# The last expert's second layer: two products of the second row block moved ahead, and the last row block computed in two column parts

## The chip, the cores and the metric

The kernel runs on one core of one Trainium2 chip. The metric is the device time of one execution in microseconds (us), taken as the median of several runs. A profile is one execution recorded by the hardware profiler; its span runs from the first to the last instruction.

## What is computed

A gated linear attention block feeds a mixture-of-experts block without dropped tokens. Cut to what matters:

```python
# attention: q, k, v, alpha of shape (4, 8, 768, 48)
state = alpha_t * state + k_t (outer) v_t ;  y_t = q_t @ state
x = y as rows: (3072, 384)

# experts: w_gate (384, 8), w1 (8, 384, 1024), w2 (8, 1024, 384)
logits = x @ w_gate ; expert_idx = argmax(logits) ; gate_w = softmax(logits)[expert_idx]
for e in range(8):                      # rows sorted by expert
    h = maximum(x_sorted[lo:hi] @ w1[e], 0.0)
    y_sorted[lo:hi] = h @ w2[e]
out = gate_w[:, None] * y_sorted[inv_perm]     # (3072, 384), float32
```

The change touches only `h @ w2[e]` of the last expert that is worked on.

## The kernel before, in words

The first part of the kernel (to about 150 us) computes the attention and routes each token to an expert. The rest goes through eight places, one expert at each. A place has a fixed number of rows: 424 less 8 for each place before it, so that the last place has 368. The experts with more tokens come first. Rows are gathered from DRAM, go through layer 1 (384 to 1024, with relu) and layer 2 (1024 to 384), and are scattered to the output by an indirect DMA on the GpSimd queue (`put`, L1080). Rows beyond a place's fixed number are dealt with in a loop at the end (L1344), which the kernel enters only if a count that it loads there is above zero.

All of this is under a manual schedule: each engine does its instructions in the order in which the code issues them, and waits are put in where data demand them.

Layer 1 (`layer1`, L948) uses a product scheme with seven products in place of eight. It works in four steps `a` of 128 columns of the hidden layer, and each step fills the hidden blocks `a` and `a + 4` of `g["h"]` (the tile `h_sb`, blocks 0 to 7). The last products, `P3` and `P4` of step 3, finish blocks 3 and 7. Their results go through VectorE (L192) and ScalarE (the relu of L978 and L982) before they are there. To have work for TensorE meanwhile, `ahead` (the `begin` of L1274) is called just before those last two products.

At places 0 to 6 the second layer uses the seven-product scheme again. The last place does it plainly, with rows as the output's partitions: blocks of 128, 128 and 112 rows (`blocks(g)`), each a sum over the eight hidden blocks `f`, with 128 columns of `h` as the stationary operand and 384 columns of `w2` as the moving one (`rows_layer2`, L1114). A float32 product of this kind is two matmul instructions with a weight load each, so that a row block has 16 of them. `ready` (L1112) lists the six hidden blocks that are there early: all but 3 and 7.

The order on TensorE at the last place:

1. The six ready products of row block 0, into a bank of the pair `pC` (tile `tp`), from `begin` (L1276).
2. `P3` and `P4` of step 3 of layer 1 (L969).
3. Hidden blocks 3 and 7 of row block 0 (L1329).
4. All eight of row block 1, into the pair `pA` (tile `sA`).
5. All eight of row block 2, into the pair `pB` (tile `sB`).

`bank` (L839) deals out PSUM banks by name, two for each name in turn. The name `y` stands for two banks that the attention used and that only the first place's early rows use later.

After each row block `scatter` (L1071) copies the sum from PSUM to a row tile `zo` (one of four buffers) and issues the put. Row blocks 0 and 1 are copied whole by ScalarE (L1077). Row block 2 is `shared`: VectorE copies the first 192 columns (L1074) and ScalarE the other 192 (L1075). Ahead of row block 0's copy, ScalarE's queue holds three copies of the place before (`z_whole`, L1106), whose puts are ahead of the last three on the GpSimd queue.

Of the kernel before, what the change touches and what calls it, by code (L numbers as in the profile page):

```python
# [8 lines left out]
F32 = mybir.dt.float32  # L9
# [11 lines left out]
def kernel(  # L21
# [29 lines left out]
    nc = tc.nc  # L51
    B, H, S, D = q.shape
    C = 128
# [4 lines left out]
    Dm = H * D  # L58
    E = moe_w_gate.shape[1]
    F = moe_w1.shape[2]  # L60
    FB = F // C
# [10 lines left out]
    NJ = 4  # L72
# [115 lines left out]
    FH = FB // 2  # L188
# [171 lines left out]
    def weights(i, layer):  # L360
        if 0 < i < E:
            ex = nc.sync.value_load(pd["xe"][0:1, i : i + 1], min_val=0, max_val=E - 1)
            groups[i][f"w{layer}"] = fetch(ex, layer)

    def blocks(g, by=1):
        return [(j, min(C, -(-(g["n"] - j * C) // by) * by)) for j in range(-(-g["n"] // C))]

    def gather(g):
        if "xg" not in g:
            g["xg"] = xg_pool.tile([C, NJ, Dm], F32, name="xg")  # L370
        for j, r in blocks(g, 16):
            nc.gpsimd.indirect_dma_start(  # L372
                out=g["xg"][:r, j, :], out_offset=None,
                in_=x_d[:, :], in_offset=bass.IndirectOffsetOnAxis(ap=g["gi"](j, r), axis=0),
            )
# [13 lines left out]
    with tc.tile_pool(name="ld", bufs=6) as ld, \  # L389
         tc.tile_pool(name="work", bufs=2) as work:  # L390
        st = {s: {} for s in range(NT)}
        y = ps.tile([C, 2, 512], F32, name="y")
# [441 lines left out]
    wk = ctx.enter_context(tc.tile_pool(name="moe_wk", bufs=1))  # L834
# [4 lines left out]
    def bank(n):  # L839
        b = banks[n]  # L840
        if len(b) < 2:
            t = pairs[n][len(b)]
            if n == "y":
                b.append(y[:, t, :])
            else:
                b.append(ps.tile([C, 512], F32, name=t, bufs=2 if t == "tp" else 1)[:])
        else:
            b.append(b.pop(0))
        return b[-1]
# [15 lines left out]
    def x_halves(g, copy=nc.scalar.copy):  # L865

        g["xt"] = wk.tile([C, NJ, 2 * DB, C], U16, name="xt")
        for j, r in blocks(g, 16):
            t = wk.tile([C, 2, Dm], U16, name="xh", bufs=4)
            copy(t[:r], g["xg"][:r, j, :].bitcast(U16).rearrange("p (c h) -> p h c", h=2))  # L870
            nc.sync.dma_start(g["xt"][:, j, :, :r], t[:r].rearrange("p h c -> p (h c)"), transpose=True)
            yield

    def x_whole(g, *js):
        if 0 in js:
            g["xT"] = wk.tile([C, DB, CAP0 + 8], F32, name="xgT")
        to = halves(g["xT"])
        for j, r in blocks(g):
            if j not in js:
                continue  # L880
            nc.scalar.copy(  # L881
                to[:, :, :, j * C : j * C + r], g["xt"][:, j].rearrange("p (h a) t -> p h a t", h=2)[:, :, :, :r],
            )
# [184 lines left out]

        return p1, rest

    def scatter(g, j, r, zp, shared=False):  # L1071
        zo = wk.tile([C, Dm], F32, name="zo", bufs=4)
        if shared:
            nc.vector.tensor_copy(zo[:r, : Dm // 2], zp[:, : Dm // 2])  # L1074
            nc.scalar.copy(zo[:r, Dm // 2 :], zp[:, Dm // 2 :])  # L1075
        else:
            nc.scalar.copy(zo[:r], zp)  # L1077
        put(g, j, r, zo)

    def put(g, j, r, zo):  # L1080
        ins = nc.gpsimd.indirect_dma_start(  # L1081
            out=out[:, :], out_offset=bass.IndirectOffsetOnAxis(ap=g["si"](j, r), axis=0),
            in_=zo[:r], in_offset=None, bounds_check=N - 1, oob_is_err=False,
        )
        if g["apart"]:
            ins = getattr(ins, "ins", ins)
            tc.declare_no_dep(ins, group="rows_out", reason="disjoint rows")
            tc.add_to_no_dep_group("rows_out", ins)
# [20 lines left out]
            )  # L1109
            put(g, j, r, zo)  # L1110

    ready = [f for f in range(FB) if f % FH < FH - 1]  # L1112

    def rows_layer2(g, j, fs):  # L1114

        r = min(C, g["n"] - j * C)
        if fs[0] == ready[0]:
            g["z"] = bank("p" + "CAB"[j])
        for f in fs:
            nc.tensor.matmul(  # L1120
                g["z"][:r, :Dm], lhsT=g["h"][:, f, j * C : j * C + r], rhs=g["w2"][:, f, :],
                start=(f == ready[0]), stop=(f == FB - 1), skip_group_check=True,
            )

    def plain(g):
# [77 lines left out]
    def early_layer2(j, fs):  # L1203

        if 0 in fs:
            eg["z"] = bank("y" if j else "pA")
        for f in fs:
            nc.tensor.matmul(
                eg["z"][:, :Dm], lhsT=eg["h"][:, f, j * C : (j + 1) * C], rhs=groups[0]["w2"][:, f, :],
                start=(f == 0), stop=(f == FB - 1),  # L1210
            )
        if FB - 1 in fs:
            yield
            scatter(eg, j, C, eg["z"][:, :Dm])
        yield

    def rest_layer1(g, beside, rows):
        n = g["n"]
        g["h"] = wk.tile([C, FB, CAP0], F32, name="h_sb")
        for f in range(FB):  # L1220
            hp = bank("p" + "CBA"[f % 3])
            for a in range(DB):
                nc.tensor.matmul(
                    hp[:, :n], lhsT=g["w1"][:, a, f * C : (f + 1) * C], rhs=g["xT"][:, a, :n],
                    start=(a == 0), stop=(a == DB - 1),
                )
            if f % 2:
                nc.vector.tensor_scalar_max(g["h"][:, f, :n], hp[:, :n], 0.0)
                next(beside, None)
            else:  # L1230
                nc.scalar.activation(g["h"][:, f, :n], hp[:, :n], AF.Relu)
                next(rows)
# [26 lines left out]
    def beside(i):  # L1259

        work = [z_halves(groups[i - 1])]
        if i == 1:
            work += [weight_sums(groups[1], 2, nc.vector)]
        while work:
            work = [w for w in work if next(w, w) is not w]
            yield

    for i, g in enumerate(groups):
        nxt = groups[i + 1] if i + 1 < E else None
        rest = []  # L1270

        last = i == E - 1

        def begin():  # L1274
            if last:
                rows_layer2(g, 0, ready)  # L1276
            else:
                p1, tail = layer2(g)
                p1()
                rest.append(tail)  # L1280

        if last:

            nc.gpsimd.drain()
        if i:
            layer1(g, beside(i), begin, last)
        else:
            rest_layer1(g, pl, x_halves(nxt))

            x_whole(nxt, 0, 1)  # L1290
            for _ in early_layer2(1, range(FH, FB)):
                pass
            x_whole(nxt, 2, 3)
            weights(1, 2)
        weights(i + 2, 1)
        if i + 2 < E:
            gather(groups[i + 2])
        if i == 0:
            for _ in x_halves(groups[2], nc.gpsimd.tensor_copy):
                pass  # L1300

        def ahead(*layers):
            if nxt:
                for layer in layers:
                    for _ in weight_sums(nxt, layer, nc.vector):
                        pass

        def turned():
            z_whole(groups[i - 1], nc.scalar.copy, 0, 1)
            yield  # L1310
            if nxt:
                row_sums(nxt)
            z_whole(groups[i - 1], nc.scalar.copy, 2)
            z_whole(groups[i - 1], nc.vector.tensor_copy, 3)
            yield
            if i + 2 < E:
                for _ in x_halves(groups[i + 2]):
                    pass
            yield

        between = turned()

        if 0 < i < E - 1:
            x_whole(nxt, *range(NJ))
        if last:
            for _ in between:
                pass
            for j, r in blocks(g):
                rows_layer2(g, j, (*([] if j == 0 else ready), FH - 1, FB - 1))  # L1329
                scatter(g, j, r, g["z"][:r, :Dm], shared=j == NJ - 2)  # L1330
        elif i:
            rest[0](lambda: ahead(*((1,) if i == E - 2 else (1, 2))), between)
        else:
            ahead(1)
            rest_layer2(g, 0)
            row_sums(nxt)
            rest_layer2(g, 1)
            rest_layer2(g, 2)
        weights(i + 2, 2)
# [4 lines left out]
    with tc.If(nx > 0):  # L1344
        with tc.For_i(0, nx, 1) as i:
# [13 lines left out]
            g = dict(n=C, w1=fetch(ex, 1), w2=fetch(ex, 2), gi=lambda j, r: gi[:, 0:1], si=lambda j, r: si[:, 0:1], apart=False)  # L1359
# [32 lines left out]
```

## Time and profile before

| | |
|---|---|
| median of 3 runs | 392.02 us (391.99 to 392.81) |
| the profiled execution's own time | 391.55 us |
| its span | 389.8 us |
| mean granted TensorE clock | 0.996 |
| instructions | 9094, of them 3378 matmuls |
| TensorE busy | 380.1 us (98% of the span) |
| VectorE, ScalarE, GpSimd busy | 210.0, 230.2, 149.2 us |

In the timeline, a row is a group of instructions that follow each other: its start, the time from the first start to the last end, engine, line, operation, output and inputs by the program's names, shapes and count; in brackets, the idle time before it and what ended that. "PE" is TensorE's matmuls, "PEld" its weight loads, which go on beside them. Matmuls are pipelined: each lasts longer than the distance between two starts, and the modelled end of the last one closes a group.

The part that the change touches begins at about 367 us of the span and ends with it.

### The profile page before, as it was taken

The page shows a single profiled execution, that of the slowest core. Times are in us where ns is not written, and L with a number is a line of the kernel's source. Part 1 is how long each engine was busy: PE and PEld are TensorE (multiplying, and loading weights), DVE is VectorE, ACT ScalarE, POOL GpSimd, SP SyncE. Part 2 cuts the span into 40 slices and gives each one's busy share as a digit, 9 for nine tenths or more (in the row PEclk, how much of TensorE's full clock was granted, in tenths as well). Part 3 has the DMA queues.
Part 4 walks back from the last instruction along what each step waited for, and adds up shares of the span by engine and source line. Part 5 has one row for each costly group of instructions (what it writes and reads, how often), then busy time and mean ns, then how long its engine had stood idle before and what let it go on. Part 6 is the DMA issues. An engine that isn't in the chain of part 4 may idle for free.

```text
span 389.8 us, 9094 instructions
## 1 busy us (share of the span) xinstructions
PE 380.1 (98%) x3378; PEld 324.1 (83%) x3378; DVE 210.0 (54%) x649; ACT 230.2 (59%) x521; POOL 149.2 (38%) x203
## 2 busy tenths in 40 slices
PE   7999999999999999999999999999999999999994
PEld 4678888888888886899889889979979979979852
DVE  5554667676676566726843663582582581552200
ACT  4576677777755431635665775675675665673540
POOL 6546464789768204257050043035025022021041
PEclk9999999999999999999999999999999999999998
DMA  8999998998994315789949459858758766801311
GB/s 169 200 201 218 203 231 194 231 218 208 244 229 136 107 42 193 149 312 250 305 117 248 85 205 235 137 197 193 188 197 206 178 203 166 157 20 38 61 63 52
DMA packets 156545, 68.08 MB, mean 175 GB/s; under 512 B 139339, under 2 KB 150722, under 8 KB 156500
## 3 DMA queue, kind: packets, MB, share of 16 engines
q1 hardware_dynamic: 151396, 57.77, 62.6%
q0 software_dynamic: 3408, 9.64, 8.3%
q8 instruction: 27, 0.44, 0.5%
q10 hardware_dynamic: 1696, 0.08, 0.3%
q14 instruction: 18, 0.15, 0.1%
HBM read 49.00 MB, written 9.58 MB: 150 GB/s over the span
## 4 chain that ended last, share of the span: by engine, by line
PE 77%; issue 15%; POOL 2%; DMA 2%; ACT 1%; DVE 1%; POOLq 0%; SPq 0%; ACTq 0%; DVEq 0%
PE tp L1051 7%; PE tp L489 6%; PE y L539 6%; PE sA L502 6%; PE x L969 4%; PE sA L969 4%; PE x L576 4%; PE sA L1034 4%; PE tp L969 3%; PE cum L969 3%; PE sB L969 3%; PE y L529 3%; PE x L1034 3%; PE tp L1034 2%; POOL out_dram L1081 2%
## 5 line engine op out<-in xcount | busy, mean ns | idle before, releaser
L1081 POOL DMA_INDIRECT out_dram<-zo,sp x25 | 26.0, 1042 | 137.5 <-ACT zo L1106 127.0
L479 POOL TENSOR_TENSOR kqb<-k_sb,icp 128x384 f32<-128x384 f32 x23 | 23.0, 1000 | 30.2 <-PE y L550 12.5
L1051 PE MATMUL tp<-h_sb,w 128*128 128x416 f32 (+5 forms) x96 | 33.9, 496 | 0.0
L502 PE MATMUL sA<-qT,kT 48*128 48x128 f32 x192 | 27.7, 284 | 0.9 <-DVE qT L493 0.9
L502 PE MATMUL sB<-qT,kT 48*128 48x128 f32 x192 | 27.7, 285 | 0.0
L372 POOL DMA_INDIRECT xg<-x_rows,gp x25 | 23.9, 954 | 10.0 <-issue 6.6
L1051 PEld LDWEIGHTS tp<-h_sb,w 128*128 128x128 f32 x96 | 18.0, 190 | 10.3 <-issue 3.7
L489 PE MATMUL tp<-ident,kqb 128*128 128x128 f32 x192 | 26.3, 280 | 0.2 <-DVE kqb L479 0.2
L502 PEld LDWEIGHTS sA<-qT,kT 48*128 48x128 f32 x192 | 23.1, 187 | 3.8 <-ACT kT L495 1.1
L980 ACT ACTIVATE h_sb<-h_sb 128x208 f32<-128x208 f32 (+6 forms) x28 | 10.3, 366 | 25.3 <-DVE h_sb L192 25.3
L192 DVE TENSOR_TENSOR h_sb<-cum,u 128x208 f32<-128x208 f32 (+6 forms) x28 | 10.1, 359 | 27.2 <-PE cum L969 20.7
L558 ACT COPY yT<-y 128x512 f32<-128x512 f32 x24 | 14.1, 587 | 17.8 <-PE y L550 7.9
L192 DVE TENSOR_TENSOR h_sb<-sB,u 128x208 f32<-128x208 f32 (+6 forms) x28 | 10.1, 359 | 26.1 <-PE sB L969 18.7
L479 POOL TENSOR_TENSOR kqb<-q_sb,cp 128x384 f32<-128x384 f32 x23 | 23.0, 1002 | 1.7 <-DMA q_sb<-in_q_dram 1.3
L969 PE MATMUL tp<-xgT,w 128*128 128x208 f32 (+6 forms) x112 | 23.1, 329 | 0.0
L489 PEld LDWEIGHTS tp<-ident,kqb 128*128 128x128 f32 x192 | 20.5, 140 | 3.2 <-issue 0.7
L502 PEld LDWEIGHTS sB<-qT,kT 48*128 48x128 f32 x192 | 23.1, 187 | 0.0
L510 DVE TENSOR_TENSOR dA<-sA,cmask 128x512 f32<-128x512 f32 x24 | 16.5, 688 | 10.2 <-PE sB L502 10.0
L195 DVE TENSOR_TENSOR th<-h_sb,th 128x208 f32<-128x208 f32 (+5 forms) x48 | 17.3, 361 | 8.1 <-ACT h_sb L982 8.1
L881 ACT COPY xgT<-xt 128x768 uint16<-128x768 uint16 (+6 forms) x25 | 20.8, 925 | 0.4 <-DMA xt<-xh 0.4
L576 PE MATMUL x<-iw,yT 128*64 128x104 f32 x368 | 20.8, 255 | 0.1
L1106 ACT COPY zo<-zr 128x768 uint16<-128x768 uint16 (+2 forms) x20 | 20.0, 1054 | 0.0
(302 smaller groups left out, 1029.0 us busy)
## 6 DMA issues: line engine op xcount, KB each, us to landing
w<-in_moe_w_dram SPq DMA_DIRECT2D x14, 1536.0 KB, 8.2
x_rows<-xs SPq DMA_DIRECT2D x24, 192.0 KB, 3.4
v_sb<-in_v_dram SPq DMA_DIRECT2D x10, 384.0 KB, 5.0
k_sb<-in_k_dram SPq DMA_DIRECT2D x9, 384.0 KB, 7.0
q_sb<-in_q_dram SPq DMA_DIRECT2D x9, 384.0 KB, 5.2
a_sb<-in_alpha_dram SPq DMA_DIRECT2D x7, 384.0 KB, 4.1
a_sb<-in_alpha_dram SPq DMA_DIRECT2D x10, 192.0 KB, 3.8
w<-in_moe_w_dram SPq DMA_DIRECT2D x6, 256.0 KB, 3.1
```

The costliest lines, as they stand in the source:

```text
L192: eng.tensor_tensor(out, a, b, op=ALU.add)
L372: nc.gpsimd.indirect_dma_start(out=g["xg"][:r, j, :], out_offset=None, in_=x_d[:, :], in_offset=bass.IndirectOffsetOnAxis(ap=g["gi"](j, r) ...
L479: eng.tensor_tensor(by_half(kq[:, i]), d[n].rearrange("s (a p) d -> s a p d", a=2), d[e][:].rearrange("s (a p d) -> s a p d", a=2, p=NP), ...
L489: nc.tensor.transpose(tp[:, p, :], pair(kqb[s % 3][:, i], p), ident[:])
L502: nc.tensor.matmul(t[:, p, :], lhsT=d["kT"][r : r + D, p, :], rhs=d["qT"][r : r + D, p, :], start=True, stop=True,)
L539: nc.tensor.matmul(yv(g)[o : o + D, j, :], lhsT=d["v"][:, g * NP + p, :], rhs=d["d" + "AB"[g]][:, p, :], start=(s < B and j == 0), stop=Tr ...
L576: nc.tensor.matmul(d["x"][o : o + HC, m, : D2 + E], lhsT=d["yT"][:, m // 2, m % 2, o : o + HC], rhs=iw[:, m, :], start=True, stop=True,)
L881: nc.scalar.copy(to[:, :, :, j * C : j * C + r], g["xt"][:, j].rearrange("p (h a) t -> p h a t", h=2)[:, :, :, :r],)
L969: nc.tensor.matmul(out, lhsT=ops[n_][0], rhs=ops[n_][1], start=first and n_ == names[0], stop=True, skip_group_check=True,)
L1034: nc.tensor.matmul(out, lhsT=lhs, rhs=rhs, start=first and f == 0, stop=True, skip_group_check=True)
L1051: nc.tensor.matmul(d2[:, :n], lhsT=w2[:, f, 2 * C :], rhs=h[:, f, :n], start=(f == 0), stop=(f == FB - 1),)
L1081: ins = nc.gpsimd.indirect_dma_start(out=out[:, :], out_offset=bass.IndirectOffsetOnAxis(ap=g["si"](j, r), axis=0), in_=zo[:r], in_offset= ...
```

## The change

- `scatter` loses its `shared` variant: every call copies the whole row block on ScalarE.
- `rows_layer2` keeps a sum for each row block (`g["z", j]` in place of `g["z"]`) and takes a bank name and a range of columns.
- At the last place, products 0 and 1 of row block 1 are issued before products 3 and 7 of row block 0; then row block 0 is copied and put, and the remaining six products of row block 1 follow.
- Row block 2 is computed in two parts: its first 256 columns into `pB` over all eight hidden blocks, copied by VectorE, and then its last 128 columns into the second bank of `y` over all eight, copied by ScalarE. Both copies go to the same `zo`, and one put follows.

```diff
-    def scatter(g, j, r, zp, shared=False):
+    def scatter(g, j, r, zp):
         zo = wk.tile([C, Dm], F32, name="zo", bufs=4)
-        if shared:
-            nc.vector.tensor_copy(zo[:r, : Dm // 2], zp[:, : Dm // 2])
-            nc.scalar.copy(zo[:r, Dm // 2 :], zp[:, Dm // 2 :])
-        else:
-            nc.scalar.copy(zo[:r], zp)
+        nc.scalar.copy(zo[:r], zp)
         put(g, j, r, zo)
...
-    ready = [f for f in range(FB) if f % FH < FH - 1]
-
-    def rows_layer2(g, j, fs):
+    late = [FH - 1, FB - 1]
+    ready = [f for f in range(FB) if f not in late]
+
+    def rows_layer2(g, j, fs, at=None, c0=0, c1=Dm):
 
         r = min(C, g["n"] - j * C)
         if fs[0] == ready[0]:
-            g["z"] = bank("p" + "CAB"[j])
+            g["z", j] = bank(at or "p" + "CA"[j])
         for f in fs:
             nc.tensor.matmul(
-                g["z"][:r, :Dm], lhsT=g["h"][:, f, j * C : j * C + r], rhs=g["w2"][:, f, :],
-                start=(f == ready[0]), stop=(f == FB - 1), skip_group_check=True,
+                g["z", j][:r, c0:c1], lhsT=g["h"][:, f, j * C : j * C + r], rhs=g["w2"][:, f, c0:c1],
+                start=(f == ready[0]), stop=(f == late[-1]), skip_group_check=True,
             )
...
         if last:
             for _ in between:
                 pass
-            for j, r in blocks(g):
-                rows_layer2(g, j, (*([] if j == 0 else ready), FH - 1, FB - 1))
-                scatter(g, j, r, g["z"][:r, :Dm], shared=j == NJ - 2)
+
+            b_ = blocks(g)
+            rows_layer2(g, 1, ready[:2])
+            rows_layer2(g, 0, late)
+            scatter(g, *b_[0], g["z", 0][: b_[0][1], :Dm])
+            rows_layer2(g, 1, ready[2:] + late)
+            scatter(g, *b_[1], g["z", 1][: b_[1][1], :Dm])
+
+            j, r = b_[2]
+            zo = wk.tile([C, Dm], F32, name="zo", bufs=4)
+            for n_, c0, c1, copy in (("pB", 0, 2 * C, nc.vector.tensor_copy), ("y", 2 * C, Dm, nc.scalar.copy)):
+                rows_layer2(g, j, ready + late, n_, c0, c1)
+                copy(zo[:r, c0:c1], g["z", j][:r, c0:c1])
+            put(g, j, r, zo)
```

More of the change, by code (lines that the diff above doesn't have):

```diff
@@ L1282 @@
         if last:
+            assert len(blocks(g)) == 3
             nc.gpsimd.drain()
```

## The prediction

> **What bounds the kernel now.** I read the page first: where the time goes, and on which engine.
>
> ```profile
> span 389.8 us, 9094 instructions
> PE 380.1 (98%) x3378; PEld 324.1 (83%) x3378; DVE 210.0 (54%) x649; ACT 230.2 (59%) x521; POOL 149.2 (38%) x203
> PEclk9999999999999999999999999999999999999998
> ```
>
> TensorE is busy for 98% of the span at full clock. So in the middle of the kernel only less TensorE work or fewer TensorE gaps count. After the last matmul it is a chain of other engines that counts. The change touches one gap and that last chain. The page's own chain ends in long "issue" pieces and says little here, so the timeline of the last 24 us is what I work from, first around the gap.
>
> ```profile
> 366.92 3.57 PEld L1120 LDWEIGHTS tp<-w,h_sb 128*128 128x128 f32 x12
> 367.07 4.03 PE L1120 MATMUL tp<-w,h_sb 128*128 128x384 f32 x12
> ...
> 371.57 0.79 PE L969 MATMUL cum<-t,w 128*128 128x184 f32 x4
> 371.77 0.33 ACT L978 ACTIVATE h_sb<-x 128x184 f32<-128x184 f32 x1 [3.71 <-PE x L969]
> ...
> 372.19 0.81 PE L1120 MATMUL tp<-w,h_sb 128*128 128x384 f32 x2
> 372.39 0.35 DVE L192 TENSOR_TENSOR h_sb<-cum,u 128x184 f32<-128x184 f32 x1 [3.95 <-PE cum L969]
> 372.78 0.51 ACT L982 ACTIVATE h_sb<-h_sb 128x368 f32<-128x368 f32 x1 [0.68 <-DVE h_sb L192]
> ...
> 373.34 0.30 PEld L1120 LDWEIGHTS tp<-w,h_sb 128*128 128x128 f32 x2 [0.95 <-ACT h_sb L982]
> 373.34 0.91 PE L1120 MATMUL tp<-w,h_sb 128*128 128x384 f32 x2 [0.34 <-ACT h_sb L982]
> ...
> 374.09 0.81 PE L1120 MATMUL sA<-w,h_sb 128*128 128x384 f32 x2
> ```
>
> The reader is to see one stall: hidden block 7 goes from the last layer-1 product (cum) through VectorE and ScalarE, whose relu ends at 372.78 + 0.51 = 373.29. TensorE has only product 3 (372.19) to fill that time, so product 7 starts at 373.34. Its stationary operand is the relu's output, so even the weight load waits. Next, the end of the kernel.
>
> ```profile
> 379.25 5.32 PE L1120 MATMUL sB<-w,h_sb 128*112 128x384 f32 x16
> 379.49 0.48 ACT L1077 COPY zo<-sA 128x384 f32<-128x384 f32 x1 [3.12 <-PE sA L1120]
> 380.25 0.99 POOL L1081 DMA_INDIRECT out_dram<-zo,sp  x1 [0.83 <-ACT zo L1077]
> 384.66 0.36 DVE L1074 COPY zo<-sB 112x192 f32<-112x192 f32 x1 [11.92 <-PEq L1344]
> 385.06 0.32 ACT L1075 COPY zo<-sB 112x192 f32<-112x192 f32 x1 [5.08 <-DVE zo L1074]
> 385.65 0.95 POOL L1081 DMA_INDIRECT out_dram<-zo,sp  x1 [4.41 <-ACT zo L1075]
> ```
>
> The two half copies run one after the other: ScalarE's is released by VectorE's. The last matmul ends at 379.25 + 5.32 = 384.57, the second copy at 385.06 + 0.32 = 385.38; so 0.81 us pass between them, and then the put, its landing and the closing of the program up to 389.8.
>
> **What the Trainium skill says.** "TensorE: Matmul & The Clock Gate", section "Step-by-step: what each phase is for", says that the next stationary operand loads while the present matmul runs. The trace agrees: in the rows above, 16 products with 16 loads take no longer than their streaming. The same page, "LDWEIGHTS (loading the stationary operand)", prices a load by its columns over 1.2, which is 107 ns for 128; the trace records 190 ns (177 for the 112 rows of block 2), and I use the distances between starts below. "PSUM — Partial Sum Buffer", "PSUM bank collisions raise a hardware error", says that two engines must not be in one bank and the same partitions at once. That is one reason for the half copies to stand in line (both read sB; they also write one zo). After the change the two copies read two banks.
>
> **Part 1, two products ahead.** Sixteen products of 384 columns take 5.32 us, of which the last takes 0.486 (a matmul's own duration in the rows of this line), so starts are (5.32 - 0.486) / 15 = 0.322 apart. From 372.19, the four instructions of products 3 and 7 would hand over to row block 1 at 372.19 + 4 x 0.322 = 373.48. It starts at 374.09: 0.61 us are lost. (0.34 are shown as idle; the rest is the drain of the product before and 0.10 of weight load in the open: 0.590 for the first product after the wait, where the others have 0.486.) With the change, products 0 and 1 of row block 1 run from 372.19 to 373.48, product 3 to 374.12, then product 7. Its weight load can start with its predecessor's start, near 373.80, half a microsecond after the relu is done. The whole 0.61 goes. The moved products need hidden blocks 0 and 1, there for long, and a bank of the pair pA: sA, whose last reader before was a relu at 366.34. So no new wait. What gets later is row block 0: done at about 374.9 in place of 374.25, but ScalarE is in three copies of the place before until 375.9, so its copy doesn't move. Row block 1 ends 0.61 earlier; its put moves from 380.25 to 379.64, behind row block 0's, which the GpSimd queue holds until 379.42: cover of 0.2, and four microseconds more before the last put. No DMA issue is moved past another, and SyncE's queue isn't touched. Gain: 0.61; if the load stayed in the open, 0.51.
>
> **Part 2, row block 2 in two parts.** It now takes 16 x 0.322 = 5.16 us. After the change it is 16 instructions of 256 columns and 16 of 128, with twice the weight loads. Both widths are in the trace elsewhere.
>
> ```profile
> 144.69 1.46 PE L671 MATMUL sB<-k_sb,w 128*128 128x256 f32 x6
> ```
>
> ```profile
> 59.83 0.82 PE L489 MATMUL tp<-ident,kqb 128*128 128x128 f32 x6
> ```
>
> ```profile
> 68.97 0.37 PE L275 MATMUL x<-pr,ones_sq 128*128 128x8 f32 x2
> ```
>
> The last of a group lasts its own duration, which each line's list gives (0.379, 0.273, 0.256). 256 columns: (1.46 - 0.379) / 5 = 0.216. 128 columns: six transposes, (0.82 - 0.273) / 5 = 0.109; but their loads are of the shorter kind (140 ns). The ordinary float32 load stands in the third row: two products of only 8 columns are 0.37 - 0.256 = 0.11 apart, so loads can follow each other at that distance. The cost of a narrow product lies between its streaming, 128 / 384 x 0.322 = 0.107 (nothing lower, as every column must pass), and 0.107 + 0.190 = 0.297, a load wholly in the open. I take 0.110. The sum is 16 x 0.216 + 16 x 0.110 = 5.22: a cost of 0.06.
>
> **Part 3, the copies.** VectorE's copy of 256 columns starts when the first part is complete. By its rows of 192 columns (0.358) and 512 (0.678) it lasts 0.42, beside the second part's 16 x 0.11 = 1.76: hidden, with over a microsecond to spare; without cover it would cost the 0.42. Behind it on VectorE stand only the load of the overflow count and the end. ScalarE's copy of 128 columns is, from 0.319 for 192 and 0.479 for 384, 0.266 long. It starts 0.08 after the last matmul, as at row block 1 (379.41 to 379.49). So 0.08 + 0.27 = 0.35 in place of 0.81: a gain of 0.46, with 0.42 to 0.50 as ends. The matmul's drain after its start distance is the same for either width (0.486 - 0.322, 0.273 - 0.109). The bank of y was last read near 166 us, and zo's buffer belonged to a put issued at 375.79, whose landing (median 2.7 us) is long past.
>
> **Part 4, after the copies.** The put follows the copy by 0.27 and takes 0.95, as before; the GpSimd queue has been idle since 381.24. "DMA: Bandwidth & Descriptors", "Anatomy of one DMA — SWDGE (gpsimd) path", puts about 2 us of fixed time on such a DMA; the trace has a median of 2.7 from issue to landing. All of that moves with the put and none of it is shortened.
>
> **Sum.** -0.61 + 0.06 - 0.46 = -1.01 us. The profiled execution took 391.55 (its span of 389.8 and 1.75 around it) and would take 390.54. The median of the runs shown is 392.02, 0.47 above it; with the same step it becomes 391.0.
>
> **Rivals.**
>
> A, *one half only*: the stall goes but the tail stays (ScalarE's copy still held back by VectorE or the new bank), or the reverse. 392.02 - 0.61 + 0.06 = 391.5, or 392.02 + 0.06 - 0.46 = 391.6. For it: the two copies share zo, and a wait for a whole tile is possible. Against it: VectorE's copy is over 1 us earlier than ScalarE's, so even that wait is met.
>
> B, *slower: the weight loads come into the open*. A narrow product streams for 0.107, less than the 0.177 that its load lasts in the record. If a load can't start before the load before it is through, or isn't hidden at all, every one of the 16 narrow products pays. Fully open: 16 x 0.177 = 2.8 us, so 392.02 - 1.07 + 2.8 = 393.8. It decides from 1.07 / 16 = 0.067 per product, a distance of 0.174. For it: loads are recorded longer than the product, and the stall above shows 0.10 of one. Against it: 0.11 for both kinds of load in the rows above.
>
> C, *no change that shows*: the tail is set by something that doesn't move, such as the landing of the last put, whose time varies. 392.0. Against it: nothing follows the last put but the program's end, and it all waits for it.
>
> **How the numbers follow.** Main case 0.82, A 0.08, B 0.05, C 0.05. By the unknown terms alone (stall 0.51 to 0.61, narrow products 0.107 to 0.112, tail 0.42 to 0.50) the main case gives 390.9 to 391.2. The three runs and the profiled one lie between 391.55 and 392.81, so a median moves by some 0.3, which makes 390.6 to 391.4. The range of 390.5 to 391.7 takes in A too; outside lie B, C and the rest of the scatter. A measurement tells 0.2% from no change, here 0.78 us, a line at 391.24. Of the main case about nine tenths lie below it (0.73), of A a quarter (0.02): faster 0.75. B counts as slower but for its mild end: 0.04. The rest, 0.21, is within 0.2%.
>
> **What would show it.** In the profile after: no wait of TensorE for the relu of L982 (0.34 before) and no gap before product 7; 16 narrow products in about 1.92 us (15 x 0.11 + 0.273), and 3.6 for the wide ones; VectorE's last copy ended before the last matmul; ScalarE's last copy ended about 0.35 after it; span near 388.8. Narrow products 0.17 or more apart would make the prediction wrong, and so would a last put that starts less than 0.8 earlier against the last layer-1 product (371.57 before).

## The result, and the profile after

The changed kernel takes 391.42 us (median of 22 runs); the kernel before takes 392.12 in the same number of runs. The ratio of the two is 0.9975, with a 95% interval of 0.9966 to 0.9983: 0.98 us less, between 0.67 and 1.33. The forecast was 1.01 less. One execution of the changed kernel took 1345.99 us, for a reason that no run shows, and the ratio leaves it out. The profiled execution took 390.48 us against 391.55, with a span of 388.8 us against 389.8.

One stretch can be compared from trace to trace without the scatter of what lies ahead of it: from the start of the last layer-1 products (four matmuls into `cum`, L969, at 371.57 before and at 371.52 after) to the end of the span. The first column of these rows is the stretch, and the number after it its length. Then come the busy time and the count of PE, PEld, VectorE (DVE), ScalarE (ACT) and GpSimd (POOL), and last the mean granted TensorE clock, the busy share of the DMA engines and the GB/s that they moved. Before:

```profile
371.57:389.82 18.25, 12.66 (x42) 6.98 (x40) 0.71 (x2) 4.72 (x8) 5.95 (x6) 0.92 0.18 61
```

After:

```profile
371.52:388.75 17.23, 12.44 (x58) 8.95 (x56) 0.78 (x2) 4.67 (x8) 5.95 (x6) 0.95 0.19 66
```

It is 1.02 us shorter. TensorE has 16 matmuls more in it, and 16 more weight loads, and is busy for less time: of the 0.61 us that the prediction counts as lost in the stall, only 0.34 were shown as idle before, and the rest stood under busy. The timeline of the changed kernel shows where the time went; first the place where the stall was.

```profile
371.52 0.79 PE L969 MATMUL cum<-t,w 128*128 128x184 f32 x4
...
372.14 1.45 PE L1117 MATMUL sA<-w,h_sb 128*128 128x384 f32 x4
372.35 0.35 DVE L192 TENSOR_TENSOR h_sb<-cum,u 128x184 f32<-128x184 f32 x1 [3.95 <-PE cum L969]
372.73 0.51 ACT L982 ACTIVATE h_sb<-h_sb 128x368 f32<-128x368 f32 x1 [0.69 <-DVE h_sb L192]
373.11 1.16 PEld L1117 LDWEIGHTS tp<-w,h_sb 128*128 128x128 f32 x4
373.14 2.85 ACT L1102 COPY zo<-zr 128x768 uint16<-128x768 uint16 x3
373.43 1.45 PE L1117 MATMUL tp<-w,h_sb 128*128 128x384 f32 x4
374.40 3.74 PEld L1117 LDWEIGHTS sA<-w,h_sb 128*128 128x128 f32 x12
...
374.72 4.03 PE L1117 MATMUL sA<-w,h_sb 128*128 128x384 f32 x12
```

The relu takes as long as before and ends at 372.73 + 0.51 = 373.24. But the two products of row block 1 (sA) now run until 373.43, and product 3 of row block 0 (tp) until 374.08, when product 7 can follow at once. No row of TensorE carries an idle time in brackets, and each group starts where its predecessor's matmuls allow: 372.14, 373.43 and 374.72 are 1.29 us apart, which is four matmuls at 0.322.

The end of the kernel, in the same timeline:

```profile
378.59 3.62 PE L1117 MATMUL sB<-w,h_sb 128*112 128x256 f32 x16
378.84 0.48 ACT L1073 COPY zo<-sA 128x384 f32<-128x384 f32 x1 [2.50 <-PE sA L1117]
379.68 0.99 POOL L1077 DMA_INDIRECT out_dram<-zo,sp  x1 [0.30 <-ACT zo L1073]
381.83 1.92 PEld L1117 LDWEIGHTS y<-w,h_sb 128*112 128x112 f32 x16
382.05 1.91 PE L1117 MATMUL y<-w,h_sb 128*112 128x128 f32 x16
382.30 0.42 DVE L1338 COPY zo<-sB 112x256 f32<-112x256 f32 x1 [9.61 <-DMA out_dram<-zo,sp]
384.04 0.27 ACT L1338 COPY zo<-y 112x128 f32<-112x128 f32 x1 [4.72 <-PE y L1117]
384.58 0.95 POOL L1077 DMA_INDIRECT out_dram<-zo,sp  x1 [3.91 <-ACT zo L1338]
```

VectorE's copy (382.30 to 382.72) lies wholly under the 128-column matmuls, which run until 382.05 + 1.91 = 383.96. (The bracket of this copy names a DMA, whose landing fell on the same moment: the put of 379.68, with the 2.6 us to its landing. The copy starts 0.09 after the last 256-column matmul, at 378.59 + 3.62 = 382.21; in split_alone below the same copy starts 0.08 after it, and there the bracket names TensorE.) Only ScalarE's copy of 0.27 us is left behind the last matmul, and it is done at 384.31, 0.35 us after it, where the two half copies took 0.80. The last put starts 13.06 us after the start of the stretch, where it was 14.08.

### The profile page after: what moved, and what is told of

Its sections match the earlier page's. It is cut to its first block, busy times and chain, and to the rows that moved or that the text cites. A ratio compares the mean times of both kernels' runs of the same rounds, so it can differ in the third digit from the quotient of the medians.

```text
span 388.8 us, 9126 instructions
## 1 busy us (share of the span) xinstructions
PE 380.0 (98%) x3394; PEld 326.1 (84%) x3394; DVE 210.4 (54%) x649; ACT 230.2 (59%) x521; POOL 149.7 (39%) x203
## 5 line engine op out<-in xcount | busy, mean ns | idle before, releaser
L969 PE MATMUL tp<-xgT,w 128*128 128x208 f32 (+6 forms) x112 | 23.1, 329 | 0.0
```

The lines of the kernel that those rows point to most:

```text
L969: nc.tensor.matmul(out, lhsT=ops[n_][0], rhs=ops[n_][1], start=first and n_ == names[0], stop=True, skip_group_check=True,)
```

## The experiments

Every kernel below was compared with the kernel before on the chip that ran it. The scatter of a whole execution is of the size of the effects, so each was also read in its trace, in the stretch defined above. The kernel before has one trace; where a kernel was traced twice, the two sums lie within 0.02 of each other. The table gives its three pieces in us: from the start of the last layer-1 products to the end of the last matmul, from there to the end of the last copy, and from there to the end of the span.

| kernel | to the last matmul | last copy | rest | sum | ratio to before (95% interval) |
|---|---|---|---|---|---|
| before | 13.00 | 0.80 | 4.45 | 18.25 | |
| changed | 12.44 | 0.35 | 4.45 | 17.23 | 0.9975 (0.9966 to 0.9983) |
| order_alone | 12.40 | 0.80 | 4.44 | 17.64 | 0.9979 (0.9967 to 0.9990) |
| split_alone | 13.04 | 0.35 | 4.45 | 17.84 | 0.9992 (0.9977 to 1.0007) |
| one_ahead | 12.44 | 0.35 | 4.46 | 17.24 | 0.9971 (0.9960 to 0.9982) |
| scalar_both | 12.44 | 0.30 | 4.45 | 17.19 | 0.9964 (0.9945 to 0.9983) |
| narrow_64 | 13.08 | 0.29 | 4.44 | 17.80 | 0.9987 (0.9976 to 0.9998) |
| two_banks_at_end | 12.44 | 0.40 | 4.70 | 17.54 | 0.9973 (0.9955 to 0.9991) |
| put_by_part | 12.44 | 0.35 | 4.06 | 16.84 | 0.9970 (0.9956 to 0.9985) |
| relu_parts | 12.80 | 0.80 | 4.43 | 18.04 | 1.0000 (0.9988 to 1.0011) |
| put_by_part_scalar | 12.44 | 0.62 | 4.05 | 17.11 | 0.9959 (0.9943 to 0.9976) |
| changed_again | 12.44 | 0.35 | 4.43 | 17.21 | 0.9967 (0.9955 to 0.9978) |
| put_by_part_2 | 12.44 | 0.35 | 4.04 | 16.83 | 0.9964 (0.9951 to 0.9977) |
| put_by_part_scalar_2 | 12.44 | 0.62 | 4.05 | 17.12 | 0.9971 (0.9957 to 0.9984) |

The theory is that of the prediction: two gains that don't depend on each other, a stall of 0.61 us filled and a copy of 0.46 hidden, less some hundredths for narrow products. The rivals are that only one of them counts, that the weight loads of narrow products come into the open, and that the last put's landing hides the tail.

**order_alone.** In the changed kernel, row block 2 whole again:

```diff
-            for n_, c0, c1, copy in (("pB", 0, 2 * C, nc.vector.tensor_copy), ("y", 2 * C, Dm, nc.scalar.copy)):
-                rows_layer2(g, j, ready + late, n_, c0, c1)
-                copy(zo[:r, c0:c1], g["z", j][:r, c0:c1])
+            rows_layer2(g, j, ready + late, "pB")
+            zp = g["z", j]
+            nc.vector.tensor_copy(zo[:r, : Dm // 2], zp[:r, : Dm // 2])
+            nc.scalar.copy(zo[:r, Dm // 2 :], zp[:r, Dm // 2 : Dm])
```

> The two products of row block 1 stand ahead, but row block 2 is computed whole and copied by VectorE and ScalarE as before. My theory: the stall for the relu is a loss of its own, so 0.61 us go between the last layer-1 product and the last matmul, and the 0.80 from the last matmul to the end of the last copy stays: -0.61 us (ratio about 0.9984). Rival, the two parts are not independent (the order brings all of it, or nothing without the split): -1.0 or 0.

Measured: the stretch is 0.61 us shorter, all of it ahead of the last matmul (13.00 to 12.40), and the copies take 0.80 as before.

```profile
373.57 0.79 PE L969 MATMUL cum<-t,w 128*128 128x184 f32 x4
...
380.64 5.32 PE L1117 MATMUL sB<-w,h_sb 128*112 128x384 f32 x16
...
386.05 0.36 DVE L1338 COPY zo<-sB 112x192 f32<-112x192 f32 x1 [11.31 <-PEq L1354]
386.45 0.32 ACT L1339 COPY zo<-sB 112x192 f32<-112x192 f32 x1 [5.08 <-DVE zo L1338]
```

The ratio stands for 0.4 to 1.3 us. The order brings its part alone.

**split_alone.** In the changed kernel, the old order:

```diff
-            rows_layer2(g, 1, ready[:2])
             rows_layer2(g, 0, late)
             scatter(g, *b_[0], g["z", 0][: b_[0][1], :Dm])
-            rows_layer2(g, 1, ready[2:] + late)
+            rows_layer2(g, 1, ready + late)
```

> Row block 2 in two column parts, but the order of before (products 3 and 7 of row block 0 first). My theory: the stall of 0.61 us stays, row block 2 takes 0.05 longer on TensorE (5.20 for 5.16, and its drain), and the last copy ends 0.35 in place of 0.80 after the last matmul: -0.41 us (ratio about 0.999). Rival, the narrow products only hide their loads because of the order: no gain or a loss. Rival, the tail is worth nothing (landing of the put): 0.

Measured: the stretch is 0.41 us shorter: 0.04 more to the last matmul and 0.46 less for the copy. The wait is back in its place, with the length it had before:

```profile
PE tp L1117 <- ACT h_sb L982: 0.3, 1, 0.3
```

That line is all that TensorE waits for in the last 25 us; the changed kernel has no such line. The ratio can't tell 0.41 us from nothing, so for this half the trace alone speaks. 0.61 + 0.41 = 1.02: the two parts add up to the whole.

**one_ahead.** One product of row block 1 ahead in place of two:

```diff
-            rows_layer2(g, 1, ready[:2])
+            rows_layer2(g, 1, ready[:1])
...
-            rows_layer2(g, 1, ready[2:] + late)
+            rows_layer2(g, 1, ready[1:] + late)
```

> The changed kernel, but only one product of row block 1 (two instructions, 0.645 us) ahead. My theory: the relu ends 1.08 us after the first product's start (372.19 to 373.29 before), the weight load of product 7 is then due after 0.97 us and its matmul after 1.29; with 0.1 of load in the open it can still start at about 1.25: no loss against the changed kernel, at most 0.05 (-1.0 us against before). Rival, the wait is met only with the load well ahead: 0.1 to 0.2 us lost against the changed kernel, and an idle time of TensorE for the relu appears.

Measured: 17.24, as the changed kernel. The timeline shows how near to the edge it is:

```profile
373.87 0.81 PE L1117 MATMUL sA<-w,h_sb 128*128 128x384 f32 x2
374.07 0.35 DVE L192 TENSOR_TENSOR h_sb<-cum,u 128x184 f32<-128x184 f32 x1 [3.96 <-PE cum L969]
374.19 0.51 PEld L1117 LDWEIGHTS tp<-w,h_sb 128*128 128x128 f32 x2
374.45 0.51 ACT L982 ACTIVATE h_sb<-h_sb 128x368 f32<-128x368 f32 x1 [0.68 <-DVE h_sb L192]
374.51 1.45 PE L1117 MATMUL tp<-w,h_sb 128*128 128x384 f32 x4
374.87 1.94 ACT L1102 COPY zo<-zr 128x768 uint16<-128x768 uint16 x2
375.01 0.34 PEld L1117 LDWEIGHTS tp<-w,h_sb 128*128 128x128 f32 x2 [0.31 <-ACT h_sb L982]
```

The weight load of product 7 does wait here (0.31 us) and starts at 375.01; its matmul isn't due before 374.51 + 2 x 0.322 = 375.15, and the four matmuls run through as one group of 1.45 us, as long as in the changed kernel. So this wait of the load cost nothing. The second product ahead adds a margin of two instructions (2 x 0.322 = 0.64 us) and brings no time.

**relu_parts.** The same wait from the other side: in the kernel before, the last relu in two instructions.

```diff
-                    nc.scalar.activation(h[:, FH + a, :n], h[:, FH + a, :n], AF.Relu)
+                    for c0, c1 in ((0, C), (C, n)) if last and a == FH - 1 else ((0, n),):
+                        nc.scalar.activation(h[:, FH + a, c0:c1], h[:, FH + a, c0:c1], AF.Relu)
```

> The kernel before, but the last relu is done in two instructions, first for the 128 rows of row block 0 and then for the rest. It has the order of before. If TensorE's stall ends with the relu of the rows that product 7 needs, the part is done 0.2 us earlier (0.31 for 0.51 us) and the kernel is 0.2 us faster. Rival, the wait is for the whole block or for ScalarE's later instruction: the two parts together last longer, 0.1 to 0.2 us slower than before.

Measured: the last matmul ends 0.20 us earlier, though the relu as a whole ends 0.09 later (1.81 after the start of the stretch, 1.72 before).

```profile
373.91 0.79 PE L969 MATMUL cum<-t,w 128*128 128x184 f32 x4
...
375.12 0.60 ACT L983 ACTIVATE h_sb<-h_sb 128x128 f32<-128x128 f32 x2 [0.68 <-DVE h_sb L192]
375.48 0.30 PEld L1121 LDWEIGHTS tp<-w,h_sb 128*128 128x128 f32 x2 [0.75 <-ACT h_sb L983]
```

Product 7's weight load starts 1.57 after the start of the stretch, where it was 373.34 - 371.57 = 1.77, and before the second part of the relu has ended (375.72). So TensorE waits for the rows that product 7 reads and not for the rest of the block. The ratio of 1.000 shows only that 0.2 us is too small for it.

**scalar_both.** Both column parts copied by ScalarE:

```diff
-("pB", 0, 2 * C, nc.vector.tensor_copy)
+("pB", 0, 2 * C, nc.scalar.copy)
```

> The changed kernel, but ScalarE copies both column parts. My theory: the gain of the tail comes from the time at which the first part is done, not from a second engine; the first copy (0.37 us) lies under the second part's 1.75 us of matmuls: as the changed kernel within 0.02 us in the trace (-1.0 us against before). Rival, two engines are what counts: 0.3 to 0.4 us slower than the changed kernel.

Measured: 17.19, 0.04 less than the changed kernel. A second engine has no part in the gain; what counts is that two thirds of the row block are complete 1.7 us ahead of the end. The 0.04 is ScalarE's start, 0.04 after the last matmul where it was 0.08. In the changed kernel a wait instruction stands on ScalarE's queue ahead of this copy (378.86 to 384.00); here the only one stands ahead of the first copy (380.36 to 383.75). That this is the reason was not tested.

**two_banks_at_end.** Two halves in two banks that end together:

```diff
+            bk = [bank("pB"), bank("y")]
+            for f in ready + late:
+                for b2, c0 in zip(bk, (0, Dm // 2)):
+                    nc.tensor.matmul(
+                        b2[:r, : Dm // 2], lhsT=g["h"][:, f, j * C : j * C + r], rhs=g["w2"][:, f, c0 : c0 + Dm // 2],
+                        start=(f == ready[0]), stop=(f == late[-1]), skip_group_check=True,
+                    )
+            nc.vector.tensor_copy(zo[:r, : Dm // 2], bk[0][:r, : Dm // 2])
+            nc.scalar.copy(zo[:r, Dm // 2 :], bk[1][:r, : Dm // 2])
```

> The changed order, but row block 2 is computed as two halves of 192 columns in two banks, one after the other for every hidden block, so that both halves end together; VectorE and ScalarE copy one each. If the half copies of before stood in line because of the common bank, they now go at once: 0.45 us from the last matmul to the last copy's end, -0.93 us against before. If the common row tile zo was the cause: 0.80 us again, -0.57 us against before.

Measured: -0.72, between the two expectations, and the timeline shows why.

```profile
384.94 0.49 PE L1339 MATMUL y<-w,h_sb 128*112 128x192 f32 x2
...
385.20 0.36 DVE L1343 COPY zo<-sB 112x192 f32<-112x192 f32 x1 [11.03 <-PE sB L1339]
385.51 0.32 ACT L1344 COPY zo<-y 112x192 f32<-112x192 f32 x1 [4.72 <-PE y L1339]
386.36 0.95 POOL L1077 DMA_INDIRECT out_dram<-zo,sp  x1 [4.23 <-ACT zo L1344]
```

ScalarE's copy is released by TensorE, no longer by VectorE, and starts at 385.51, before VectorE's copy has ended (385.56). Both write the same zo, so the common zo does not make copies stand in line. What is left for the kernel before is the common bank, as the Trainium skill's "PSUM — Partial Sum Buffer", section "PSUM bank collisions raise a hardware error", would have it: two engines may not be in one bank on the same partitions at once. (The tile sB went with the bank; no run has one of the two without the other.) The copies are done 0.40 after the last matmul. But then 0.26 is lost again: the put starts 0.53 after the last copy, where every other run here has 0.27. The copies end at 385.56 and 385.83, 0.27 apart. In the changed kernel, where the put needs two copies too, they end 1.6 us apart; in the kernel before ScalarE's copy waits for VectorE's. That the put waits longer because both ends are new to GpSimd's queue was not tried.

**narrow_64.** The cut at 320 and 64 columns:

```diff
-("pB", 0, 2 * C, nc.vector.tensor_copy), ("y", 2 * C, Dm, nc.scalar.copy)
+("pB", 0, Dm - 64, nc.vector.tensor_copy), ("y", Dm - 64, Dm, nc.scalar.copy)
```

> The changed kernel, but row block 2 is cut at 320 and 64 columns in place of 256 and 128. My theory: products can't follow each other closer than their weight loads allow, about 0.11 us, whatever their width; so 16 x 0.269 + 16 x 0.11 = 6.06 us in place of 5.20, and the last copy is 0.05 shorter: 0.8 us slower than the changed kernel (some -0.2 us against before). Rival, only the columns that stream count: 64 columns take 0.054, the sum stays at 5.17, 0.1 us faster than the changed kernel.

Measured: 0.57 us slower than the changed kernel in the trace. Neither number was met; the direction is the theory's, the size was not.

```profile
380.25 4.47 PE L1117 MATMUL sB<-w,h_sb 128*112 128x320 f32 x16
384.29 1.82 PEld L1117 LDWEIGHTS y<-w,h_sb 128*112 128x112 f32 x16
384.56 1.70 PE L1117 MATMUL y<-w,h_sb 128*112 128x64 f32 x16
384.81 0.49 DVE L1338 COPY zo<-sB 112x320 f32<-112x320 f32 x1 [10.46 <-PE sB L1117]
386.33 0.21 ACT L1338 COPY zo<-y 112x64 f32<-112x64 f32 x1 [5.36 <-PE y L1117]
```

Matmuls of 64 columns start 0.098 us apart (the loads' group shows it: 16 of them in 1.82 us, of which the last takes 0.178 and the first gap, still under a 320-column matmul, 0.27; so (1.82 - 0.178 - 0.27) / 14 = 0.098). Their streaming alone would be 64 / 384 x 0.322 = 0.054. So the columns that stream do not set the distance. The loads go at the same 0.098, and the 0.11 of the prediction came from loads of 128 columns, where these have 112: 112 / 128 x 0.11 = 0.096. That fits a floor set by the loads, of 0.098 and not of 0.11; it is argued from these two widths, and no run has the same narrow product with another load. The Trainium skill's "TensorE: Matmul & The Clock Gate", section "LDWEIGHTS (loading the stationary operand)", prices a load by its columns over 1.2, which is 93 ns for 112; the trace is 5% above that. The change's own cut at 128 columns, with 0.109 between starts, is just on the free side: its streaming (0.107) is longer than 0.098.

**put_by_part.** A row tile and a put of its own for each column part; `put_part` is `put` with the column at which the part begins:

```diff
-            zo = wk.tile([C, Dm], F32, name="zo", bufs=4)
             for n_, c0, c1, copy in (("pB", 0, 2 * C, nc.vector.tensor_copy), ("y", 2 * C, Dm, nc.scalar.copy)):
+                zo = wk.tile([C, Dm], F32, name="zo", bufs=4)
                 rows_layer2(g, j, ready + late, n_, c0, c1)
                 copy(zo[:r, c0:c1], g["z", j][:r, c0:c1])
-            put(g, j, r, zo)
+                put_part(g, j, r, zo[:r, c0:c1], c0)
```

> The changed kernel, but each column part of row block 2 has a row tile and an indirect put of its own: the 256 columns are put while the 128 are computed, and the last put moves a third of the bytes. My theory: the last put's issue costs the same 0.95 us, and from its end to the landing some 0.2 to 0.5 us go, since the packets of the last put took 0.8 us before: -1.3 us against before. Rival, a put's time from issue to landing is fixed and doesn't depend on its bytes: as the changed kernel (-1.0). Second rival, the earlier put holds the queue (0.95 and 0.3 between puts) beyond the last copy: slower than the changed kernel by up to 0.3.

Measured: 16.84, 0.39 us less than the changed kernel, all of it in the rest after the last copy (4.45 to 4.06). The DMA view of the last put alone gives packets, MB and share of the engines; the changed kernel:

```profile
q0 software_dynamic: 64, 0.15, 9.5%
```

put_by_part:

```profile
q0 software_dynamic: 34, 0.05, 4.4%
```

The issue is no shorter (0.95 us each). What shrinks is the time from there to the end of the program, with a third of the bytes and about half the packets on the way; the run does not tell bytes and packets apart. The Trainium skill's "DMA: Bandwidth & Descriptors", section "Anatomy of one DMA — SWDGE (gpsimd) path", has about 2 us fixed and the bytes over 436 GB/s; for the 98 KB less (147.6 to 49.3 in the trace, where one packet of 3 KB in put_by_part's view is still the earlier put's) an estimate from it is 0.23 us, and 0.39 was measured. The earlier put does not hold the queue:

```profile
384.80 0.95 POOL L1087 DMA_INDIRECT out_dram<-zo,sp  x1 [2.33 <-DVE zo L1347]
385.83 0.27 ACT L1347 COPY zo<-y 112x128 f32<-112x128 f32 x1 [4.72 <-PE y L1126]
386.37 0.95 POOL L1087 DMA_INDIRECT out_dram<-zo,sp  x1 [0.62 <-ACT zo L1347]
```

It ends at 385.75, and the last put could go 0.3 after it; it is ScalarE's copy that it waits for.

**put_by_part_scalar and changed_again.** The last two edits together, and the changed kernel once more on the same chip:

```diff
-("pB", 0, 2 * C, nc.vector.tensor_copy)
+("pB", 0, 2 * C, nc.scalar.copy)
```

> Two of the edits tried so far, together: a put of its own for each column part, and both copies on ScalarE. If the gains seen in the traces (0.39 us from the last put's start to the end, 0.045 between the last matmul and the last copy) add up, the tail from the start of the last layer-1 product takes 16.8 us, 1.46 less than before and 0.44 less than the changed kernel. Rival, the first put, which now waits for ScalarE as the last one does, is late enough to hold the queue: no gain over the changed kernel.

> The changed kernel itself once more, on the chip of the kernel above, as its measure: 1.0 us below before in all theories, and the tail from the start of the last layer-1 product 17.24 us as in its first profile.

Measured: changed_again has 17.21, as expected. The sum of the two gains is missed: 17.11 in place of 16.8. The put keeps its gain (4.05), but ScalarE's last copy starts 0.36 us after the last matmul in place of 0.04 to 0.08. The next runs ask whether that is of the program.

**put_by_part_2 and put_by_part_scalar_2.** Both once more, on one chip.

> The kernel with a put for each column part once more, beside its variant with both copies on ScalarE, on one chip. Theory: 16.84 us from the start of the last layer-1 product to the end as in its first profile, 1.4 below before (ratio about 0.9964), and 0.4 below the changed kernel's 17.24.

> A put for each part and both copies on ScalarE, once more. In its first profile ScalarE's last copy started 0.36 us after the last matmul, where 0.04 to 0.08 was seen elsewhere. If that was of this one execution, 16.8 us from the start of the last layer-1 product to the end; if the program brings it (one more wait ahead of the copy on ScalarE's queue), 17.1 again, and the variant with VectorE is the better one by 0.3.

Measured: 16.83 and 17.12; the late copy came again to the hundredth, so it belongs to the program. In the timeline of put_by_part_scalar_2 the last matmul ends at 385.21 + 1.91 = 387.12, and the copy starts at 387.48; its bracket names TensorE's queue (PEq):

```profile
385.21 1.91 PE L1126 MATMUL y<-w,h_sb 128*112 128x128 f32 x16
385.45 0.37 ACT L1347 COPY zo<-sB 112x256 f32<-112x256 f32 x1 [2.98 <-PE sB L1126]
386.10 0.95 POOL L1087 DMA_INDIRECT out_dram<-zo,sp  x1 [2.28 <-ACT zo L1347]
387.48 0.27 ACT L1347 COPY zo<-y 112x128 f32<-112x128 f32 x1 [1.65 <-PEq L1362]
```

Its cause stays open. ScalarE has one wait more ahead of this copy than in scalar_both, for a row tile of its own. But put_by_part has that wait ahead of the same copy, and the copy starts 0.08 after the last matmul there, so the wait alone is not the cause. The wait instruction itself ends at 387.16, 0.04 after the last matmul, and 0.32 pass from there to the copy, where put_by_part has 0.04. What differs is that ScalarE has done the first copy 1.65 us before; no run takes that apart. The best version tried is put_by_part, with VectorE for the first part: in its two traces 0.39 us below the changed kernel. In whole runs (0.9970 and 0.9964) its interval overlaps the changed kernel's (0.9975 and 0.9967), so that the 0.39 rests on the traces.

## Why the prediction was right

*Part 1, the stall.* Predicted a gain of 0.61, with no new wait of TensorE: order_alone has 0.61, and relu_parts shows that the relu was what TensorE waited for. That row block 0's copy would not move is seen too (375.90 before and 375.86 after, in traces that are 0.05 apart), and row block 1's put starts at 379.68, where 379.64 was worked out. That is nearer than the reasoning deserves: the trace after starts 0.05 earlier, so the put is 0.09 late. Row block 0's put ends at 378.37 + 1.01 = 379.38, and puts that follow each other at once stand 0.30 apart; the "cover of 0.2" left that out. It costs nothing, as the next put is nearly 4 us later. Both products were moved; one_ahead shows that one would have done, which the prediction didn't ask.

*Part 2, the narrow products.* Predicted 0.06 more, measured 0.04: 0.216 and 0.109 between starts, where 0.216 and 0.110 were taken. Rival B (loads in the open, 0.174 and more) is refuted at this width. narrow_64 has products of 64 columns 0.098 apart, far from their streaming of 0.054, so that a limit of the kind that B names lies close by.

*Part 3, the copies.* Predicted 0.46, measured 0.46 (0.80 to 0.35, unrounded 0.804 to 0.347). The hidden copy lasts 0.42 as worked out and ends 1.2 us before the last matmul. The prediction named the common bank and the common tile as possible reasons for the line of the half copies; two_banks_at_end rules out the tile zo, which leaves the bank.

*Part 4, after the copies.* Predicted to move and not to shrink: 4.45 before and after. Rival C (the landing hides the tail) is refuted by split_alone's trace, where the copies end 0.46 earlier and the rest stays at 4.45. put_by_part adds that the landing is on the path: the smaller last put shortens the span.

*Rival A, one half only:* the two halves alone give 0.61 and 0.41, together 1.02.

*The base.* 391.0 was forecast on a median of 392.02 and 391.42 was measured. Of the 0.4 between them, 0.1 is the base (392.12 in 22 runs) and 0.3 is the step of the medians: 0.70, where the means (391.33 without the long execution, and 392.31) are 0.98 apart and the traces 1.02. So no term of the sum is shown to be off by that much; it fits the scatter of the runs. The prediction gave 0.75 to a gain of more than 0.2%. Measured is 0.25%, with 0.17% to 0.34% as its interval, so this is not decided. That the profiled executions differ by 1.07, near the forecast, is in part luck: the stretch starts at anything from 371.5 to 374.7 us in the traces here, and in these two within 0.05.

## What to carry to other kernels

When an engine's last wait is for a short chain on other engines, count what is ready from the next block: here 0.645 us of independent work was enough, and a weight load that waited 0.31 us cost nothing, since its matmul was not yet due. At the end of a program, cut the last block so that the larger part is complete, copied and sent while the smaller is computed. Don't cut too narrow: here 64 columns lost 0.57 us against 128. With a third of the bytes in the last put, what is behind the copy was 0.39 us shorter. Where an effect is of the size of the scatter, measure it in a stretch of the trace that starts at a fixed instruction: two traces of one kernel agreed within 0.02 us here, where the intervals of whole runs were 0.3 us and more to either side.

## What was not expected of the hardware

A matmul of 64 columns with a fresh 112-column float32 load follows the one before by 0.098 us, less than the 0.11 that 128-column loads had shown, as a floor would that goes with the columns loaded. A put whose two sources were complete 0.27 us apart started 0.53 after the last copy in place of 0.27. ScalarE's last copy in put_by_part_scalar started 0.36 after the last matmul in both executions, in place of 0.04 to 0.08. Of the last two the cause is open.
